# One more group of tokens by Strassen's products in a fused sliding attention and ReLU-squared kernel

## The chip, the cores and the metric

The kernel runs on one core of a Trainium2 chip. The metric is device time in microseconds of one execution; lower is better. Three runs of the kernel before gave 291.15, 291.99 and 292.82 us, a median of 291.99.

## The reference

Attention with a sliding window of 128 and a bias that falls off linearly with distance, over 8 batches, 8 heads, 576 positions and head size 64; then, on the 4608 tokens of 512 features that come out, a two-layer network with a squared ReLU between the layers.

```python
scores = scale * np.matmul(q, k.transpose(0, 1, 3, 2))
mask = (rel >= 0) & (rel < window)
scores = np.where(mask, scores + bias[None], -1000000000.0)
attn = np.exp(scores)
attn = attn / (np.sum(attn, axis=-1, keepdims=True) + 1e-09)
x = np.matmul(attn, v)
h = x @ w_in
r = np.maximum(h, 0.0)
g = r * r
return (g @ w_out).astype(np.float32)
```

## The kernel before

**Tiling.** The sequence of a batch is cut into 5 blocks of 128 positions (the last has 64), 40 blocks in all, numbered b0 to b39. A block's keys and queries are loaded as `kq`, turned by TensorE (`tp`, L483) or by a DMA into `kqT`, multiplied into scores (`ps_s`, L533 and L552), put through the exponential by ScalarE (`E`, L598), masked by VectorE (`P`, L609), multiplied with the values (`pv`, L639), normalised by VectorE (`rec`, `x`), and turned again (`xp`, L698) into `xT`, features by tokens. The 4608 tokens are also cut into 9 groups of 512. Group g can be worked on when its tokens stand in `xT`: group 1, tokens 512 to 1023, needs blocks b4 to b8.

**The network, direct form.** Up: `fc_step` (L745) multiplies slices of `w_in_sb` with the group's tokens into a bank `h`; ScalarE makes the ReLU `rt`, then VectorE or ScalarE the square `g`. Group 0 does so in slices of 128 tokens, group 1 in slices of 256 (`SPLIT`). Down: `plain` (L1054), for group 0 alone, 64 matmuls of 512 columns over `w_out_sb`.

**The network by Strassen's algorithm** (in the form with 7 products and 15 sums). The groups in `FAST`, 2 to 8, do their up-projection in `fast_unit` (L820): four units, one for each quarter of `w_in`, each with 7 products of 4 matmuls of 256 columns into banks `f`. It needs sums of quarters of `w_in` (`weight_sums`, L392: `w_sum`, made once) and of the group's tokens (`token_sums`, L789: `T`, and one of them in place in `xT`). In a unit ScalarE copies product 1 out (`fs`), VectorE adds that to product 6 in its bank (L886), ScalarE copies the sum out (`fu`), and only then may product 7 write that bank; it is copied out as `fx`. VectorE adds `fx` or `fu` to banks to give three quarters of the result (L854). Groups 1 to 8 do their down-projection so as well, in `product` (L975), with sums of quarters of `w_out` (`w_mix`, L377) and of `g` (`S`, L934).

**The order of the work** is made by a planner before the program is built. Each piece of work has a cost, the work it depends on, the buffers it takes and frees, and a key; the planner takes, engine by engine, what can start first, and by the key where several can. `SPREAD` shifts the keys by random draws. The engines then run their instructions strictly in that order. The keys of the first two groups count up from 0; of the loads, the order is written out in `FIRST` (b a block, i a quarter of `w_in`, o a quarter of `w_out`) and moved a little by draws with a negative share. POOL issues all loads (L429 blocks, L360 `w_in`, L367 `w_out`), SP all stores (L1043, L1021) and the transposes by DMA.

**The end.** For the last group the third result bank is two banks, one for each half of the rows, so that the last product (number 7, `halves`) can run one half after the other; each half has its addition (L1015) and its store of 128 x 256 (L1021).

## Time and profile before

| | us |
|---|---|
| median of three runs | 291.99 |
| the profiled execution | 291.18 |
| its span, first instruction to last | 289.2 |
| TensorE busy in the span | 281.6 |
| VectorE busy | 256.1 |
| ScalarE busy | 229.1 |
| POOL busy | 107.6 |

The page is one execution. Engines are PE (TensorE), PEld (its weight loads), DVE (VectorE), ACT (ScalarE), POOL and SP. A group of instructions has its line in the kernel, what it writes and reads, how many there are, their busy time, the mean duration of one in ns, and the idle time of the engine just before them with what ended it. Durations of neighbours on an engine can overlap by some tens of ns. The chain that ended last is followed back from the last instruction, at each step to what released it or to the instruction ahead of it on its engine.

### The profile page before, as it was taken

The page shows a single profiled execution, that of the slowest core. Times are in us where ns is not written, and L with a number is a line of the kernel's source. Part 1 is how long each engine was busy: PE and PEld are TensorE (multiplying, and loading weights), DVE is VectorE, ACT ScalarE, POOL GpSimd, SP SyncE. Part 2 cuts the span into 40 slices and gives each one's busy share as a digit, 9 for nine tenths or more (in the row PEclk, how much of TensorE's full clock was granted, in tenths as well). Part 3 has the DMA queues.
Part 4 walks back from the last instruction along what each step waited for, and adds up shares of the span by engine and source line. Part 5 has one row for each costly group of instructions (what it writes and reads, how often), then busy time and mean ns, then how long its engine had stood idle before and what let it go on. Part 6 is the DMA issues. An engine that isn't in the chain of part 4 may idle for free.

```text
span 289.2 us, 9480 instructions
## 1 busy us (share of the span) xinstructions
PE 281.6 (97%) x3869; PEld 239.2 (83%) x3869; DVE 256.1 (89%) x625; ACT 229.1 (79%) x470; POOL 107.6 (37%) x134
## 2 busy tenths in 40 slices
PE   8899999999999999999999999999999999999995
PEld 6788878865788888888988888888888888888884
DVE  6876879999798999998999999989999988998823
ACT  6659888995489985999899989898879888588420
POOL 8958676944672516332634245332000000000000
PEclk9999999999999999999999999999999999999999
DMA  9999999999999999999999999999234101201223
GB/s 135 160 179 174 172 180 186 155 126 208 191 191 141 150 126 192 161 161 110 226 158 126 127 197 157 164 177 158 37 101 70 47 20 61 86 0 39 74 75 109
DMA packets 165867, 38.36 MB, mean 133 GB/s; under 512 B 153024, under 2 KB 165312, under 8 KB 165824
## 3 DMA queue, kind: packets, MB, share of 16 engines
q0 software_dynamic: 114704, 18.10, 92.3%
q1 hardware_dynamic: 50064, 19.41, 35.8%
q8 instruction: 30, 0.49, 0.7%
q10 hardware_dynamic: 1056, 0.26, 0.4%
q14 instruction: 13, 0.11, 0.1%
HBM read 36.70 MB, written 9.44 MB: 160 GB/s over the span
## 4 chain that ended last, share of the span: by engine, by line
PE 88%; POOL 4%; DMA 3%; DVE 2%; ACT 1%; issue 0%; DVEq 0%
PE o L975 33%; PE f L820 30%; PE h L745 8%; PE pv L639 6%; PE o L1054 5%; DMA w_in_sb<-in_moe_w_in_dram 3%; PE ps_s L533 3%; POOL kq L429 2%; PE ps_s L552 2%; POOL vt L429 1%; PE tp L483 1%; POOL w_in_sb L360 1%; PE xp L698 1%; DVE rt L854 1%; DVE g L869 0%
## 5 line engine op out<-in xcount | busy, mean ns | idle before, releaser
L429 POOL DMA_DIRECT2D vt<-in_v_dram x40 | 34.1, 854 | 66.5 <-PE pv L639 58.1
L598 ACT ACTIVATE E<-ps_s 128x384 bf16<-128x384 f32 (+2 forms) x114 | 50.5, 508 | 8.6 <-PE ps_s L533 8.6
L975 PEld LDWEIGHTS <-g 128*128 128x128 bf16 x512 | 49.1, 98 | 6.0
L820 PEld LDWEIGHTS <-w_sum 128*128 128x128 bf16 x448 | 43.1, 97 | 6.3 <-issue 0.5
L609 DVE TENSOR_TENSOR P<-E,masks 128x1024 bf16<-128x1024 bf16 (+1 forms) x67 | 43.5, 656 | 2.5 <-ACT E L598 1.6
L429 POOL DMA_DIRECT2D kq<-in_k_dram x39 | 33.2, 851 | 24.9 <-DMA kqT<-kq 17.5
L975 PEld LDWEIGHTS <-S 128*128 128x128 bf16 x384 | 36.6, 98 | 4.5 <-issue 0.4
L848 ACT ACTIVATE rt<-f 128x512 bf16<-128x512 f32 x56 | 33.2, 600 | 6.8 <-PE f L820 6.6
L975 PE MATMUL o<-w_out_sb,g 128*128 128x256 bf16 x256 | 38.3, 273 | 0.0
L975 PE MATMUL o<-w_mix,g 128*128 128x256 bf16 x256 | 37.2, 273 | 0.0
L745 PE MATMUL h<-xT,w_in_sb 128*128 128x128 bf16 (+1 forms) x384 | 35.3, 237 | 1.2 <-issue 0.6
L975 PE MATMUL o<-w_mix,S 128*128 128x256 bf16 x256 | 36.1, 273 | 0.2 <-ACT E L598 0.2
L820 PEld LDWEIGHTS <-w_in_sb 128*128 128x128 bf16 x336 | 31.8, 97 | 4.4
L820 PE MATMUL f<-xT,w_in_sb 128*128 128x256 bf16 x224 | 34.6, 273 | 0.0
L429 POOL DMA_DIRECT2D kq<-in_q_dram x39 | 33.4, 857 | 2.6 <-PE h L745 1.3
L871 ACT ACTIVATE g<-rt 128x512 bf16<-128x512 bf16 x52 | 32.6, 634 | 1.7 <-DVE rt L859 0.9
L820 PE MATMUL f<-xT,w_sum 128*128 128x256 bf16 x224 | 33.5, 272 | 0.2 <-DVE rt L854 0.2
L672 DVE TENSOR_TENSOR x<-pv,rec 128x256 bf16<-128x256 f32 (+1 forms) x80 | 33.0, 415 | 0.4
L820 PE MATMUL f<-T,w_sum 128*128 128x256 bf16 x224 | 32.1, 273 | 0.0
L639 PE MATMUL pv<-vt,P 128*128 128x65 bf16 x576 | 30.8, 193 | 0.9 <-DVE P L609 0.9
L639 PEld LDWEIGHTS <-P 128*128 128x128 bf16 x576 | 25.7, 97 | 6.1 <-DVE P L609 2.0
L745 PEld LDWEIGHTS <-w_in_sb 128*128 128x128 bf16 x384 | 26.7, 98 | 3.7 <-issue 1.0
(78 smaller groups left out, 504.1 us busy)
## 6 DMA issues: line engine op xcount, KB each, us to landing
out_dram<-osb SPq DMA_DIRECT2D x35, 256.0 KB, 3.7
vt<-in_v_dram POOLq DMA_DIRECT2D x32, 128.0 KB, 5.5
kq<-in_k_dram POOLq DMA_DIRECT2D x31, 128.0 KB, 6.0
kq<-in_q_dram POOLq DMA_DIRECT2D x31, 128.0 KB, 6.3
w_out_sb<-in_moe_w_out_dram POOLq DMA_DIRECT2D x4, 512.0 KB, 9.6
w_in_sb<-in_moe_w_in_dram POOLq DMA_DIRECT2D x6, 256.0 KB, 7.9
kq<-in_k_dram POOLq DMA_DIRECT2D x8, 64.0 KB, 5.7
kq<-in_q_dram POOLq DMA_DIRECT2D x8, 64.0 KB, 6.2
```

Of the source, the lines that this page charges most:

```text
L429: nc.gpsimd.dma_start(o, src[b, :, kb * 128:kb * 128 + n, :].rearrange("h s d -> s h d"))
L533: nc.tensor.matmul(sl.tile[lo:lo + 64, at:at + w], k[rows, c, unit:unit + 64], own[rows, C + c, q0:q0 + w], start=True, stop=True)
L598: nc.scalar.activation(o, src, AF.Exp, bias=0.0, scale=scale)
L609: nc.vector.tensor_tensor(Pt[sP.idx][:, hs, p0:2, 0:n], e, masks[:, hs, p0:2, 0:n], op=ALU.mult)
L639: nc.tensor.matmul(slot_v.tile[:, hi * (D + 1):(hi + 1) * (D + 1)], Pt[sP.idx][:, place(h), part, :], vt[s_in[mk, "v"].idx][:, h, :], star ...
L672: nc.vector.tensor_tensor(xt[sx.idx][0:n, hf * 256:(hf + 1) * 256].rearrange("p (h e) -> p h e", h=4), pv[0:n, :, 0:D], srec.tile[0:n, :]. ...
L745: nc.tensor.matmul(slot.tile[:, f * w:(f + 1) * w], w_in_sb[:, cc, (fc + f) * 128:(fc + f + 1) * 128], xT[:, cc, g * 512 % RING + lo:g * 5 ...
L820: nc.tensor.matmul(bank[name].tile[:, jj * 256:jj * 256 + 256], w, m, start=opens and jj == 0 and k == 0, stop=k == 1, skip_group_check=True)
L848: nc.scalar.activation(srt.tile, bank[name].tile, AF.Relu, bias=0.0, scale=1.0)
L871: nc.scalar.activation(o, i, AF.Square)
L975: nc.tensor.matmul(bank[t].tile[:, t * 256:(t + 1) * 256], left(g, what, j)[:, t * 128:(t + 1) * 128], right(by, j), start=opens and j == ...
L1054: nc.tensor.matmul(bank.tile, g_slots[g].tile[:, fc, t * 128:(t + 1) * 128], w_out_sb[:, fc], start=fc == 0, stop=fc == FCB - 1)
```

## The change

Group 1 joins `FAST`: its up-projection takes the seven products too, 112 matmuls of 256 columns for 128 of 256. Its token sums and units stand at the keys where its `fc_step` calls stood, and the weight sums ahead of them, where before they stood behind group 0. A weight sum is one instruction of 512 columns; it was two of 256. For the last group the third result bank is three banks (of the planner's class `z` the third): rows 0 to 127 with 256 columns, rows 128 to 255 with two times 128 columns. Products 5 and 7, which write them, have 24 matmuls each for 16, product 7 piece after piece, and each piece has its addition and store. `SPREAD` has other draws, 14 for 11, so that work of all groups is ordered anew.

```diff
--- before.py
+++ after.py
@@ -227,7 +227,7 @@
     EARLY = 0.92
     WIDE = NKB
     SQUARES = 352.0
-    FAST = range(NG - 7, NG)
+    FAST = range(NG - 8, NG)
     RING = 4 * 512
     HALVED = (0, 1, 2)
 
@@ -265,7 +265,7 @@
 
     plan = Plan({"rec": 4, "rt": 3, "g": 2, "S": 2, "S2": 1, "osb": 4,
                  "s1": 1, "u2": 1, "x1": 1, "fs": 1, "fu": 2, "fx": 1, **size},
-                {"h": 3, "o": 3, "a": 4, "f": 5, "t": 3})
+                {"h": 3, "o": 3, "a": 4, "f": 5, "t": 3, "z": 1})
 
     def bank_tile(sl, name, dtype=FP32):
         return psum.tile([128, 512 if dtype == FP32 else 1024], dtype, tag=f"bank{sl.idx}", bufs=1, name=name)
@@ -388,9 +388,8 @@
         for o, a, b, op in ((s1, a21, a22, ALU.add), (s2, s1, a11, ALU.subtract),
                             (s3, a11, a21, ALU.subtract), (s4, a12, s2, ALU.subtract)):
             def emit(o=o, a=a, b=b, op=op):
-                for k in range(2):
-                    nc.vector.tensor_tensor(o[:, k], a[:, k], b[:, k], op=op)
-            last = plan.add({"DVE": 2 * dve(256, 2)}, key, emit, [t_win[n][-1], last, t_read[1][0]])
+                nc.vector.tensor_tensor(o, a, b, op=op)
+            last = plan.add({"DVE": dve(512, 2)}, key, emit, [t_win[n][-1], last, t_read[0 if 1 in FAST else 1][0]])
         t_wsum[n] = last
 
     s_in, t_in = {}, {}
@@ -958,7 +957,7 @@
     def product(g, i, key):
         what, by, where = PRODUCTS[i]
         if i == 0:
-            KEEP[g] = {"bank": [[Slot("o")] * 2, [Slot("o")] * 2, [Slot("o"), Slot("o")] if g == NG - 1 else [Slot("o")] * 2],
+            KEEP[g] = {"bank": [[Slot("o")] * 2, [Slot("o")] * 2, [Slot("o"), Slot("o"), Slot("z")] if g == NG - 1 else [Slot("o")] * 2],
                        "last": None, "t": [None] * 3,
                        "s1": Slot("s1"), "u2": Slot("u2"), "x1": Slot("x1")}
         kp = KEEP[g]
@@ -967,27 +966,32 @@
         apart = bank[0] is not bank[1]
         last = kp["last"]
         halves = i == 6 and g == NG - 1
-        for j, t in ([(j, t) for t in range(2) for j in range(FCB // 2)] if halves
-                     else [(j, t) for j in range(FCB // 2) for t in range(2)]):
-                def emit(j=j, t=t):
-                    if opens and j == 0 and (t == 0 or apart):
-                        bank[t].tile = bank_tile(bank[t], "o")
-                    nc.tensor.matmul(bank[t].tile[:, t * 256:(t + 1) * 256],
-                                     left(g, what, j)[:, t * 128:(t + 1) * 128], right(by, j),
-                                     start=opens and j == 0 and (t == 0 or apart), stop=j == FCB // 2 - 1,
+        parts = [(0, 0, 256), (1, 0, 128), (1, 128, 256)] if apart else [(0, 0, 256), (1, 0, 256)]
+        done_at = []
+        for j, x in ([(j, x) for x in range(len(parts)) for j in range(FCB // 2)] if halves
+                     else [(j, x) for j in range(FCB // 2) for x in range(len(parts))]):
+                t, lo, hi = parts[x]
+
+                def emit(j=j, x=x, t=t, lo=lo, hi=hi):
+                    if opens and j == 0 and (x == 0 or apart):
+                        bank[x].tile = bank_tile(bank[x], "o")
+                    nc.tensor.matmul(bank[x].tile[:, t * 256 + lo:t * 256 + hi],
+                                     left(g, what, j)[:, t * 128:(t + 1) * 128], right(by, j)[:, lo:hi],
+                                     start=opens and j == 0 and (x == 0 or apart), stop=j == FCB // 2 - 1,
                                      skip_group_check=True)
+                t = x
                 new = j == 0 and t == 0
                 here = [bank[t]] if opens and j == 0 and (t == 0 or apart) else []
-                end = i == 6 and j == FCB // 2 - 1 and t == 1
-                if halves and j == 0 and t == 1:
-                    half_done = last
+                end = i == 6 and j == FCB // 2 - 1 and t == len(parts) - 1
                 if what[0] == "s":
                     needs = [t_sum[g, j // 4]]
                 else:
                     needs = [q for lo, hi, q in g_sq[g][2 * j + (what != "a11")]]
-                last = plan.add({"PE": mm(256)}, key(i * 16 + 2 * j + t), emit,
+                last = plan.add({"PE": mm(hi - lo)}, key(i * 16 + 2 * j + t), emit,
                                 [last, (t_wmix if by[0] == "t" else t_wout)[j // 2], kp["t"][where] if new else None] + needs,
                                 here, [g_slots[g], s_slots[g][0]] if end else [s_slots[g][1]] if i == 1 and j == FCB // 2 - 1 and t == 1 else [])
+                if j == FCB // 2 - 1:
+                    done_at.append(last)
         kp["last"] = last
         k = key(i * 16 + 15)
 
@@ -1008,17 +1012,17 @@
                 copy(te, f32(so.tag, so, plan.bufs[so.tag]), bank[0].tile)
             te = plan.add({"ACT": act(512), "DVE": dve(512)} if i in BOTH else {"ACT": act(512)}, k, keep, [done_], [so], free)
         elif halves:
-            for t, dep in ((0, half_done), (1, last)):
+            for x, (t, lo, hi) in enumerate(parts):
                 so = Slot("osb")
 
-                def plus(t=t, so=so):
-                    nc.vector.tensor_tensor(f32("osb", so, plan.bufs["osb"])[:, 0:256], bank[t].tile[:, t * 256:t * 256 + 256],
-                                            kp["u2"].tile[:, t * 256:t * 256 + 256], op=ALU.add)
-                te = plan.add({"DVE": dve(256)}, k, plus, [dep, kp["from", "u2"]], [so], [bank[t], kp["u2"]])
-
-                def store(t=t, so=so):
+                def plus(x=x, lo=t * 256 + lo, hi=t * 256 + hi, so=so):
+                    nc.vector.tensor_tensor(f32("osb", so, plan.bufs["osb"])[:, 0:hi - lo], bank[x].tile[:, lo:hi],
+                                            kp["u2"].tile[:, lo:hi], op=ALU.add)
+                te = plan.add({"DVE": dve(hi - lo)}, k, plus, [done_at[x], kp["from", "u2"]], [so], [bank[x], kp["u2"]])
+
+                def store(t=t, lo=lo, hi=hi, so=so):
                     r0 = g * 512 + t * 128
-                    nc.sync.dma_start(out[r0:r0 + 128, 256:512], so.tile[:, 0:256])
+                    nc.sync.dma_start(out[r0:r0 + 128, 256 + lo:256 + hi], so.tile[:, 0:hi - lo])
                 plan.add({"SP": 350.0}, k, store, [te], [], [so], dma=1040.0)
             return
         else:
@@ -1026,11 +1030,11 @@
             add = kp[{4: "x1", 6: "u2"}[i]]
 
             te = None
-            for lo, hi in ((0, 256), (256, 512)) if apart else ((0, 512),):
-                def plus(lo=lo, hi=hi):
+            for x, (lo, hi) in enumerate(((0, 256), (256, 384), (384, 512)) if apart else ((0, 512),)):
+                def plus(x=x, lo=lo, hi=hi):
                     if lo == 0:
                         f32(so.tag, so, plan.bufs[so.tag])
-                    nc.vector.tensor_tensor(so.tile[:, lo:hi], bank[lo // 256].tile[:, lo:hi], add.tile[:, lo:hi], op=ALU.add)
+                    nc.vector.tensor_tensor(so.tile[:, lo:hi], bank[x].tile[:, lo:hi], add.tile[:, lo:hi], op=ALU.add)
                 te = plan.add({"DVE": dve(hi - lo)}, k, plus, [te, last, kp["from", add.tag]], [so],
                               free + [add])
         kp["t"][where] = te
@@ -1068,13 +1072,20 @@
 
     key = 0
     for g in range(2):
-        for lo, hi in SPLIT[g]:
+        if g in FAST:
+            for n in range(4):
+                weight_sums(n, key + 14 * n - 12)
+            t_of = token_sums(g, key)
+            for n in range(4):
+                fast_unit(g, n, key + 16 * n, t_of)
+            key += 64
+        for lo, hi in SPLIT[g] if g not in FAST else []:
             for fc in range(0, FCB, 512 // (hi - lo)):
                 fc_step(g, fc, key, lo, hi)
                 key += 4
     for g in range(NG):
         base = key
-        if g == 1:
+        if g == 1 and 1 not in FAST:
             for n in range(4):
                 weight_sums(n, base + 64 * n)
         if g and g + 1 in FAST:
@@ -1096,8 +1107,9 @@
             if g * 512 < lo + blk[kb] and g * 512 + 512 > lo:
                 t.deps += t_read[g]
 
-    SPREAD = ((78, 3, 1), (425, 16, 0.01), (451, 8, 0.01), (463, 8, 0.03), (537, 3, 0.1), (602, 1.5, -0.15),
-              (705, 3, 0.03), (1454, 16, 0.03), (1463, 3, -0.15), (1578, 3, 0.03), (1611, 3, 0.01))
+    SPREAD = ((9504, 3, 1), (9631, 8, 0.01), (9673, 8, 0.1), (9696, 3, 0.03), (9736, 8, 0.1), (9741, 3, 0.03),
+              (9777, 3, 0.03), (9891, 3, -0.15), (9976, 8, 0.03), (10008, 3, 0.01), (10013, 16, 0.03),
+              (10071, 3, 0.01), (10091, 16, 0.01), (10181, 16, 0.01))
     work_of = sorted({t.group for t in plan.tasks if t.group[1] > -100000})
     load_of = sorted({t.group for t in plan.tasks if t.dma and -900000 < t.group[1] < -800000})
     shift = dict.fromkeys(work_of + load_of, 0.0)
```

**The order, POOL, the loads after block b3.** Names: `w_in_sb` 128x4x512 is a whole quarter of `w_in`, here the last; `kq_71`, `vt_79` with 64 rows are b4, `kq_72`, `vt_80` are b5, `kq_73` b6. Before:

```order
L360 DMA w_in_sb<-in_moe_w_in_dram 128x2x512 x2
L429 DMA kq_71<-in_k_dram 64x8x64
L429 DMA kq_71<-in_q_dram 64x8x64
L429 DMA vt_79<-in_v_dram 64x8x64
L429 DMA kq_72<-in_k_dram 128x8x64
L429 DMA kq_72<-in_q_dram 128x8x64
L429 DMA vt_80<-in_v_dram 128x8x64
L360 DMA w_in_sb<-in_moe_w_in_dram 128x4x512
L429 DMA kq_73<-in_k_dram 128x8x64
```

Now:

```order
L360 DMA w_in_sb<-in_moe_w_in_dram 128x2x512 x2
L360 DMA w_in_sb<-in_moe_w_in_dram 128x4x512
L428 DMA kq_71<-in_k_dram 64x8x64
L428 DMA kq_71<-in_q_dram 64x8x64
L428 DMA vt_79<-in_v_dram 64x8x64
L428 DMA kq_72<-in_k_dram 128x8x64
L428 DMA kq_72<-in_q_dram 128x8x64
L428 DMA vt_80<-in_v_dram 128x8x64
L428 DMA kq_73<-in_k_dram 128x8x64
```

The last quarter of `w_in` moved ahead of the six loads of b4 and b5.

**The order, PE, behind the last transpose of block b8's result** (`xp` from `x_2_89`), with which group 1's tokens are complete. Before, group 1's direct matmuls follow:

```order
L698 LDWEIGHTS x_2_89
L698 MATMUL xp_1303<-ident_64,x_2_89 128x128
L745 LDWEIGHTS w_in_sb_66
L745 MATMUL h_1274<-xT_69,w_in_sb_66 128x256
L745 LDWEIGHTS w_in_sb_66
L745 MATMUL h_1274<-xT_69,w_in_sb_66 128x256
```

Now, matmuls of group 0's down-projection follow (`g_480` is group 0's `g`):

```order
L697 LDWEIGHTS x_2_89
L697 MATMUL xp_1276<-ident_64,x_2_89 128x128
L1058 LDWEIGHTS g_480
L1058 MATMUL o_1075<-w_out_sb_67,g_480 128x512
L1058 LDWEIGHTS g_480
L1058 MATMUL o_1075<-w_out_sb_67,g_480 128x512
```

Of group 0's 64 matmuls of 512 columns 42 now stand ahead of group 1's first product, and the eleventh behind this place is the first to need the last quarter of `w_out`. Before, 7 of the 64 stood ahead of group 1's first direct matmul, and the other 57 behind 104 or more of its 128.

**The order, DVE, around the normalisation of block b3** (`x_89`). Now weight sums stand among it; before, the first stood behind the first `w_mix`:

```order
L671 TENSOR_TENSOR x_89<-pv,rec 128x256
L661 RECIPROCAL rec<-pv 128x4
L391 TENSOR_TENSOR w_sum<-w_in_sb 128x2x256
L671 TENSOR_TENSOR x_89<-pv,rec 128x256
L766 TENSOR_TENSOR g<-rt 128x4x128
L391 TENSOR_TENSOR w_sum<-w_sum,w_in_sb 128x2x256
L442 COPY xT<-xp 128x4x128
L391 TENSOR_TENSOR w_sum<-w_in_sb 128x2x256 x2
```

The sums of the first quarters moved from the middle of group 1's direct form to the time of b3's attention.

## The prediction

> **What bounds the kernel now.** I read the page first, busy time and the 40 slices, then the chain that ended last, then that chain in order of time.
>
> ```profile
> PE 281.6 (97%) x3869; PEld 239.2 (83%) x3869; DVE 256.1 (89%) x625; ACT 229.1 (79%) x470; POOL 107.6 (37%) x134
> PEclk9999999999999999999999999999999999999999
> PE 88%; POOL 4%; DMA 3%; DVE 2%; ACT 1%; issue 0%; DVEq 0%
> ```
>
> TensorE is busy for 97% of the span at full clock and is 88% of the chain. A busy PE can still be slowed by pauses between pipelined matmuls, so I look at the pace inside long runs of the chain in order of time (start, length, what, how many):
>
> ```profile
> 29.10 1.34 PE h L745 x24
> 33.17 0.47 PE ps_s L533 x32
> 55.85 0.45 PE tp L483 x8
> 74.15 1.51 PE o L1054 x7
> 80.15 0.48 PE pv L639 x16
> 249.83 2.18 PE f L820 x20
> 270.07 15.62 PE o L975 x143
> ```
>
> A matmul of 256 columns takes 2.18 / 20 = 0.109 us, one of 128 columns 1.34 / 24 = 0.056, one of 512 columns 1.51 / 7 = 0.216, a transpose 0.056, a pv 0.030, a block's scores 0.47. The last 143 matmuls run at 15.62 / 143 = 0.109 without a gap. So PE is bound by its own work almost everywhere, and a matmul saved is worth its full 0.109 us, if what feeds PE keeps up. The second engine by load is VectorE. The stretches tell where each has room (us, then busy time with counts of PE, PEld, DVE, ACT, POOL, clock, DMA share, GB/s):
>
> ```profile
> 10.00:20.00 10.00, 9.25 (x194) 8.36 (x188) 7.12 (x19) 6.91 (x14) 7.31 (x10) 1.00 1.53 171
> 20.00:30.00 10.00, 9.52 (x210) 8.50 (x208) 7.26 (x18) 8.64 (x19) 8.63 (x11) 1.00 1.90 175
> 30.00:40.00 10.00, 9.37 (x202) 7.95 (x199) 7.83 (x23) 8.57 (x17) 6.92 (x9) 1.00 1.93 176
> 40.00:50.00 10.00, 10.00 (x160) 8.72 (x152) 8.95 (x27) 8.64 (x18) 6.18 (x8) 1.00 1.66 187
> 50.00:60.00 10.00, 10.00 (x150) 7.70 (x148) 10.00 (x37) 9.75 (x21) 8.99 (x11) 1.00 2.37 148
> 60.00:80.00 20.00, 20.00 (x257) 13.13 (x255) 17.62 (x51) 12.80 (x30) 9.35 (x12) 1.00 1.92 180
> 150.00:200.00 50.00, 49.78 (x708) 42.87 (x706) 48.90 (x114) 45.82 (x98) 18.33 (x22) 1.00 1.58 160
> ```
>
> Before 40 us PE has small holes while loads arrive; from 40 us it has none. VectorE is 98% busy from 150 to 200 us and PE still loses only 0.22 us there.
>
> **The eighth up-projection: PE.** Group 1 leaves the direct form, 128 matmuls of 256 columns, and takes Strassen's, 7 products x 4 units x 4 = 112 matmuls of 256 columns. The 16 that go are worth 16 x 0.109 = **-1.74 us**, the only large gain in the change.
>
> **The same: VectorE and ScalarE.** The forms with their mean durations (line, engine, operation, count | busy us, mean ns | idle before):
>
> ```profile
> L886 DVE TENSOR_TENSOR f<-f,fs 128x512 f32<-128x512 f32 x28 | 19.2, 687 | 1.4 <-ACT fs L880 1.4
> L854 DVE TENSOR_TENSOR rt<-f,fx 128x512 bf16<-128x512 f32 x28 | 19.2, 685 | 4.4 <-ACT fx L901 4.0
> L859 DVE TENSOR_SCALAR rt<-rt 128x512 bf16<-128x512 bf16 x28 | 9.2, 330 | 0.6
> L789 DVE TENSOR_TENSOR T<-xT 128x512 bf16<-128x512 bf16 x7 | 2.9, 418 | 0.0
> L392 DVE TENSOR_TENSOR w_sum<-w_in_sb 128x256 bf16<-128x256 bf16 x16 | 3.7, 280 | 0.0
> L880 ACT ACTIVATE fs<-f 128x512 f32<-128x512 f32 x28 | 17.0, 606 | 2.4 <-PE f L820 2.1
> L890 ACT ACTIVATE fu<-f 128x512 f32<-128x512 f32 x28 | 16.8, 599 | 3.6 <-DVE f L886 3.5
> ```
>
> Four units add 4 additions into the bank (0.687), 8 additions that make rt (0.685), some 3 more ReLUs of rt (0.330), and 4 token sums (0.418): 2.7 + 5.5 + 1.0 + 1.7 = 10.9 us, and about two squares more, 0.8. That is 11.7 us of VectorE, all between about 40 and 80 us. What goes from there are the weight sums, 32 x 0.280 = 9.0 us, which stand between 47 and 72 us. Net +2.7 us. The idle time of VectorE in those 40 us is 40 - 8.95 - 10.00 - 17.62 = 3.4, so it ends at 98%, as it is from 150 to 200 us. ScalarE gets 12 copies of 0.60, 7.2 us, and has 40 - 8.64 - 9.75 - 12.80 = 8.8 idle; that is covered.
>
> The price of a full VectorE is paid where PE waits for the chain copy fs, addition, copy fu: 0.606 + 0.687 + 0.599 = 1.89 us, before the bank may take product 7. Beside it stand products 5 and 2 (8 x 0.109 = 0.87) and whatever attention lies between. The lower bound is the 0.22 us that the like stretch from 150 to 200 loses; the upper one is one whole chain, 1.9, since the four units share what is between them. I take **+0.7**, nearer to the low end, because that stretch runs the same chains at the same load.
>
> **The weight sums, wider and sooner.** They are 16 of 512 columns now. By the token sums' row of the same size (418 ns) that is 6.7 us, ahead of 40 us, where VectorE idles 2.88 + 2.74 + 2.17 = 7.8 us. They cost nothing as long as these holes cover them. If a mask or a normalisation comes late behind them, each costs PE up to its own 0.42; I leave it at 0, with up to 1 in the range.
>
> **The loads.** All go through POOL's one queue, in order.
>
> ```profile
> w_in_sb<-in_moe_w_in_dram POOLq DMA_DIRECT2D x1, 512.0 KB, 7.3
> L367 POOL DMA_DIRECT2D w_out_sb<-in_moe_w_out_dram x4: 772/780/792, 26.6 to 39.3; - x4
> DMA to landing us min/median/max: 8.5/9.6/10.3
> 40.59 0.39 PE L483 MATMUL tp<-ident,kq 128*128 128x128 bf16 x4
> ```
>
> The last quarter of w_in passes six loads of blocks 4 and 5. Half a megabyte at 175 GB/s is 3.0 us, so these blocks land up to 3 us later. PE's cover: ahead of block 4's transposes stand, by the order of both, 159 of group 0's h matmuls in place of 128, 31 x 0.056 = 1.7 us. What is missing, up to 1.3 us, is not lost for good, because PE now meets a later gate. Group 0's down-projection (64 matmuls of 512 columns) stands ahead of group 1's first matmul, 42 of the 64, and needs all of w_out. In both orders the second half of block 8's transposes is at the same place; in the trace it starts at 40.59 and leaves PE free at 40.81. From there to the first matmul that needs w_out's last quarter stand 28 of 512 columns, 32 pv, one block's scores (and 0.1 to drain them) and 12 transposes: 6.05 + 0.96 + 0.57 + 0.67 = 8.25 us, so PE arrives at 49.1. That quarter is issued at 39.3 and lands 8.5 to 10.3 us later, at 47.8 to 49.6. The wait is 0 to 0.5; I take **+0.5**, because that load is the last of a full queue. Before, direct h matmuls filled this time, and nothing waited.
>
> **The last product in three pieces.**
>
> ```profile
> L1033 DVE TENSOR_TENSOR osb<-o,u 128x512 f32<-128x512 f32 x7 | 4.7, 674 | 0.0
> L1015 DVE TENSOR_TENSOR osb<-o,u 128x256 f32<-128x256 f32 x2 | 0.8, 424 | 0.6 <-PE o L975 0.6
> out_dram<-osb SPq DMA_DIRECT2D x2, 128.0 KB, 1.8
> ```
>
> For the last group, products 5 and 7 (L975) trade 16 matmuls of 256 columns for 32 of 128: 32 x 0.056 - 16 x 0.109 = **+0.05**. After the last matmul stands an addition of 128 columns; halving 512 to 256 saves 0.25, so halving again saves half of that, **-0.13**. The store behind it is 64 KB: between nothing saved and half of 1.8, I take **-0.15**, since fixed parts of a transfer stay.
>
> The Trainium skill speaks against these pieces: TensorE: Matmul & The Clock Gate, Back-to-back issue gap, puts a stream of load and matmul pairs at about 81 ns for 128 columns, and 131 for 512. The trace disagrees twice, with 56 and 216. By that figure the pieces would cost 32 x 0.081 - 16 x 0.109 = +0.85, an estimate from that page, in place of +0.05.
>
> **Sum.** -1.74 + 0.7 + 0.5 + 0.05 - 0.13 - 0.15 = -0.77 us. The profiled execution took 291.18 (span 289.2 and 2.0 around it), so its like would take 290.4. The median of the three runs, 291.99, is 0.8 above that execution; from it the sum gives 291.2. I forecast the middle, **290.8**.
>
> **Rivals.**
>
> 1. **The covers hold everywhere: faster.** The waits of 0.5 and 0.7 come to nothing: -1.97, and the new draws, which reorder all groups, may take away some of the waits in the later part. In the middle of the two starting points that is 291.6 - 2.0 = 289.6. For it: every matmul saved lies on PE's chain, and PE loses almost nothing at 98% VectorE. Against it: the gate at 49 us did not exist before.
> 2. **VectorE becomes the bound: slower.** Over the whole run it gets 11.7 more and 9.0 - 6.7 = 2.3 less, 9.4 us, while PE gets shorter. It decides if from 40 us on the additions come more than about one chain (1.9 us) behind PE: then what does not fit into 3.4 us is carried into stretches that are already 98% busy, and PE waits at every unit. If half of the 9.4 shows, +4.7 - 2.0 = +2.7: 294.3. Against it: ScalarE can take squares and ReLUs.
> 3. **PE is bound by the queue of loads until 50 us, so the matmuls saved are not seen**, as blocks 4 to 6 and then w_out arrive when they arrive: the saving of 1.74 shrinks to the tail's 0.2: 291.4. For it: loads arrive one behind another there. Against it: group 1's up-projection, where the saving is, lies behind that gate.
> 4. The pace of 81 ns for 128 columns, by the page's rule: 291.6; the rows of 56 ns speak against it.
>
> **How the numbers follow.** Chances: forecast 0.37, rival 1 0.38, rival 2 0.14, rival 3 0.09, rival 4 0.02. What a measurement of this kernel tells from no change is about 0.5%, 1.46 us, so faster is below 290.5 and slower above 293.4. The forecast's own range is 289.9 to 291.9, by the bounds of its two waits and the two starting points, and counts as the same, near the edge. With rivals 3 and 4 the same has 0.48, faster 0.38, slower 0.14. The range that leaves out 2 in 10 goes from 289.2, rival 1 with some of the later waits gone, to 292.7, part of rival 2's way.
>
> **What would show it.** In the changed profile PE should have some 3869 matmuls (16 fewer for f and h, 16 more for o), VectorE's busy time some 9 us more, the weight sums before 35 us. A wait of PE for w_out near 49 us shows the gate; PE's f waiting for ACT fu between 50 and 75 us shows the chain; if both are missing and the time is under 290, rival 1 holds. Busy VectorE of 10 in every stretch from 40 to 100 us with PE under 9.9 shows rival 2. The forecast is wrong at its root if a run of 20 f matmuls no longer takes 2.18 us, or if PE from 40 to 270 us loses more than 2 us.

## The result, and the profile after

The changed kernel takes 296.25 us (median of four runs, 295.77 to 297.06) against 291.75 for the kernel before on the same chip: a ratio of 1.0155 with an interval of 1.0126 to 1.0184. It is slower by 4.5 us. The forecast was 290.8, no change, and the time lies above its range.

The page of the changed kernel: span, busy time, VectorE's 40 slices, and the chain that ended last by engine and by line.

```profile
span 295.3 us, 9476 instructions
PE 283.9 (96%) x3862; PEld 239.2 (81%) x3869; DVE 266.0 (90%) x632; ACT 231.8 (78%) x477; POOL 107.8 (37%) x134
...
DVE  6797989899999999999999899989999988989823
...
PE 54%; DVE 19%; ACT 11%; DMA 7%; POOL 5%; issue 2%; ACTq 0%
PE o L978 24%; PE f L819 20%; DMA w_out_sb<-in_moe_w_out_dram 4%; DMA w_in_sb<-in_moe_w_in_dram 3%; DVE rt L853 3%; DVE P L608 3%; PE pv L638 3%; POOL kq L428 3%; PE o L1058 3%; ACT g L870 2%; DVE S L933 2%; DVE x L671 2%; DVE f L885 2%; ACT E L597 2%; POOL vt L428 2%
```

TensorE's part of the chain fell from 88% to 54%, and VectorE, which had 2%, has 19%. TensorE's busy share hardly moved (97% to 96%), so the page says who has become critical but not where. The stretches say where. Columns as in the prediction: us, length, then busy time and count of PE, PEld, DVE, ACT, POOL, then clock, DMA share, GB/s. First the kernel before, in two stretches that it was not shown in above:

```profile
40.00:57.00 17.00, 17.00 (x251) 14.58 (x243) 15.95 (x52) 15.39 (x32) 12.55 (x16) 1.00 1.98 174
57.00:86.00 29.00, 29.00 (x387) 20.28 (x384) 26.45 (x77) 21.15 (x45) 16.37 (x21) 1.00 1.88 179
```

and the same stretches of the changed kernel:

```profile
40.00:57.00 17.00, 15.60 (x191) 9.65 (x194) 14.90 (x40) 6.74 (x14) 12.20 (x15) 1.00 1.82 182
57.00:86.00 29.00, 26.68 (x417) 20.24 (x419) 28.48 (x69) 26.72 (x59) 15.48 (x19) 1.00 2.06 152
```

From 40 to 57 us PE has lost 1.4 us of busy time, and ScalarE works less than half of what it did (6.74 for 15.39): it has nothing to do. From 57 to 86 us PE has lost 2.3, VectorE has 0.5 us left of 29 and ScalarE 2.3. So there are two places, a hungry one and a crowded one.

PE's busy time hides part of the loss, since a matmul that drains alone still counts as busy. So I also followed how far PE lags: the start of a matmul, less the work of all matmuls ahead of it at the paces of the prediction (0.109 us for 256 columns, 0.056 for 128, 0.216 for 512, 0.030 for a pv, 0.015 to 0.024 for a score; 0.083 for each of the 28 warm-up matmuls, which only shifts the points). Some records are missing from the traces, and not evenly. All 64 weight loads of group 0's down-projection (512 columns) are there in each, but behind them the kernel before has 64 matmuls, the changed one 57 and e1 to e14 56 to 58, and the gaps lie between 37 and 76 us. Each would add its 0.216 us to the lag, 1.3 to 1.7 us in all, to every kernel but the one before. So one matmul is put back behind each weight load that has none (in e7 two of its `h` as well). With them the changed kernel has the 3869 that the prediction named, and the stretches above have some 0.2 us more of PE in the first and 0.4 in the second. Lag in us, at that much work done; e1 is the changed kernel profiled again:

| work done, us | 10 | 30 | 45 | 60 | 70 | 100 | lag added 30 to 45 | 45 to 60 | 60 to 70 |
|---|---|---|---|---|---|---|---|---|---|
| before | 6.96 | 9.52 | 9.86 | 10.15 | 10.38 | 11.74 | 0.34 | 0.29 | 0.23 |
| changed | 7.98 | 10.35 | 12.65 | 14.11 | 17.61 | 18.44 | 2.30 | 1.46 | 3.50 |
| e1 | 8.57 | 12.51 | 13.80 | 15.22 | 18.79 | 19.61 | 1.29 | 1.42 | 3.57 |

In the changed kernel 30, 45, 60 and 70 us of work are reached at 40, 58, 74 and 88 us, so the first of the three differences is the hungry place and the other two are the crowded one. About 1 us of lag is there at the start. The hungry place adds 1 to 2 us more than before (0.9 of the 2.30 falls right at the point 30, and e1 has 1.29), the crowded place 4.4, and from there the changed kernel loses no more than the one before. At 100 us of work it is 6.7 us behind; PE's saving of 1.74 us stands against that, which leaves 5.0 beside the 4.5 measured.

What happens in the first place concerns group 1's matmuls. Here is the plain form of the kernel before, in a view by shape from 36 to 45 us, and the Strassen form of the changed one, the products on sums of tokens, in the view of the bank's tile from 40 to 60 us (count, duration ns min/median/max, first and last start, shape):

```profile
L745 PE MATMUL h<-xT,w_in_sb 128*128 128x256 bf16 x28 | 4.0, 273 | 0.0
```

```profile
L819 PE MATMUL f<-T,w_sum x14: 272/273/273, 54.0 to 59.6; 128*128 128x256 bf16 x14
```

By 45 us the kernel before has done 28 of group 1's matmuls, on the first 256 of its 512 tokens (`SPLIT`). A unit of Strassen's form waits for the sums of tokens, which mix both halves, so it needs all 512; the first product on such sums starts at 54.0. Until then PE takes group 0's down-projection, and ScalarE waits for work. In the second place the waits, from 60 to 90 us (who waited for whom: us in total, times, longest):

```profile
PEld L638 <- DVE x L671: 1.4, 2, 0.9
...
PE pv L638 <- DVE x L671: 1.0, 2, 0.6
...
PEld L697 <- DVE x L671: 0.9, 2, 0.4
...
PE f L819 <- DVE x L671: 0.6, 1, 0.6
```

PE waits for VectorE's attention rows, and the chain in order of time (start, length, what) shows why these are late:

```profile
80.10 0.69 DVE P L608
80.79 0.60 DVE S L933
81.39 0.33 DVE xT L442
81.73 0.60 DVE S L933
82.32 0.34 DVE T L788
82.66 0.60 DVE g L933
83.26 0.34 DVE T L788
83.60 0.60 DVE S L933
84.20 0.34 DVE xT L788
84.53 0.33 DVE x L671
...
85.29 0.58 DVE P L608
85.87 0.34 DVE x L671
86.21 0.05 issue
86.26 0.42 PE pv L638 x8
```

In this chain VectorE runs without a gap. Sums for the next products (S, g, T) stand between two masks P, and the pv that PE waits for comes 6 us after the first of them.

### The profile page after: what moved, and what is told of

Its sections match the earlier page's. It is cut to its first block, busy times and chain, and to the rows that moved or that the text cites. A ratio compares the mean times of both kernels' runs of the same rounds, so it can differ in the third digit from the quotient of the medians.

```text
span 295.3 us, 9476 instructions
## 1 busy us (share of the span) xinstructions
PE 283.9 (96%) x3862; PEld 239.2 (81%) x3869; DVE 266.0 (90%) x632; ACT 231.8 (78%) x477; POOL 107.8 (37%) x134
## 4 chain that ended last, share of the span: by engine, by line
PE 54%; DVE 19%; ACT 11%; DMA 7%; POOL 5%; issue 2%; ACTq 0%
PE o L978 24%; PE f L819 20%; DMA w_out_sb<-in_moe_w_out_dram 4%; DMA w_in_sb<-in_moe_w_in_dram 3%; DVE rt L853 3%; DVE P L608 3%; PE pv L638 3%; POOL kq L428 3%; PE o L1058 3%; ACT g L870 2%; DVE S L933 2%; DVE x L671 2%; DVE f L885 2%; ACT E L597 2%; POOL vt L428 2%
## 5 line engine op out<-in xcount | busy, mean ns | idle before, releaser
L819 PEld LDWEIGHTS <-w_sum 128*128 128x128 bf16 x512 | 49.0, 98 | 8.1 <-issue 0.9
L847 ACT ACTIVATE rt<-f 128x512 bf16<-128x512 f32 x64 | 38.0, 599 | 9.0 <-PE f L819 7.4
L819 PEld LDWEIGHTS <-w_in_sb 128*128 128x128 bf16 x384 | 36.6, 97 | 6.3 <-issue 1.4
L819 PE MATMUL f<-xT,w_in_sb 128*128 128x256 bf16 x256 | 40.7, 272 | 0.6 <-DVE x L671 0.6
L870 ACT ACTIVATE g<-rt 128x512 bf16<-128x512 bf16 x61 | 38.4, 636 | 2.4 <-DVE rt L858 1.5
L819 PE MATMUL f<-xT,w_sum 128*128 128x256 bf16 x256 | 39.6, 272 | 0.4 <-DVE rt L853 0.2
L819 PE MATMUL f<-T,w_sum 128*128 128x256 bf16 x256 | 39.2, 273 | 0.0
L978 PE MATMUL o<-w_mix,S 128*128 128x256 bf16 (+1 forms) x264 | 37.9, 269 | 0.0
L868 DVE TENSOR_TENSOR g<-rt 128x512 bf16<-128x512 bf16 x67 | 27.8, 420 | 3.5 <-ACT rt L847 1.4
L853 DVE TENSOR_TENSOR rt<-f,fx 128x512 bf16<-128x512 f32 x32 | 21.9, 684 | 4.0 <-ACT fx L900 3.7
```

The source lines that it names most:

```text
L819: nc.tensor.matmul(bank[name].tile[:, jj * 256:jj * 256 + 256], w, m, start=opens and jj == 0 and k == 0, stop=k == 1, skip_group_check=True)
L847: nc.scalar.activation(srt.tile, bank[name].tile, AF.Relu, bias=0.0, scale=1.0)
L853: nc.vector.tensor_tensor(srt.tile, bank[name].tile, add.tile, op=ALU.add)
L868: nc.vector.tensor_tensor(o, i, i, op=ALU.mult)
L870: nc.scalar.activation(o, i, AF.Square)
L978: nc.tensor.matmul(bank[x].tile[:, t * 256 + lo:t * 256 + hi], left(g, what, j)[:, t * 128:(t + 1) * 128], right(by, j)[:, lo:hi], start=o ...
```

## The experiments

The order of rows is made by the planner, and anything that changes its tasks also deals the draws anew. So some runs below keep the changed kernel's order and only make work smaller, and others drop the draws or replace them, and compare partners. e1 to e8 ran on one chip, e9 and e10 on a second and e11 to e14 on a third, where the kernel before took 291.1 to 291.3, 292.6 and 291.6 us. So between these three sets the ratios to the kernel before are compared, not the times.

**e1, the changed kernel again.**

> The changed kernel once more, beside its variants. All theories: 296 us, 4 to 5 above the kernel before. Its second profile tells whether two things in the first one are of the program or of that execution: the load of w_in's second half that landed 1.2 us later than before (15.9 for 14.8), and block b8's queries that took 1.9 us in the queue where a like load takes 0.9. If they are of the program, b8's queries land at 42 again; if of the execution, near 41.

296.55 us, ratio 1.0170 (1.0128 to 1.0213). It is the base of the next three.

**e2, the second group's additions on 64 columns.**

```diff
-                    nc.vector.tensor_tensor(srt.tile, bank[name].tile, add.tile, op=ALU.add)
+                    w = 64 if g == 1 else 512
+                    nc.vector.tensor_tensor(srt.tile[:, 0:w], bank[name].tile[:, 0:w], add.tile[:, 0:w], op=ALU.add)
+                    if g == 1:
+                        nc.vector.memset(srt.tile[:, w:512], 0.0)
...
-            nc.vector.tensor_tensor(bank["B"].tile, bank["B"].tile, fs.tile, op=ALU.add)
+            nc.vector.tensor_tensor(bank["B"].tile[:, 0:w], bank["B"].tile[:, 0:w], fs.tile[:, 0:w], op=ALU.add)
```

> The changed kernel, same order, but group 1's additions into the bank and its additions that make rt work on 64 of 512 columns (rt's rest is set to zero), so its numbers are wrong for that group. That takes 12 x 0.6 us from VectorE between 50 and 86 us and gives back about 12 x 0.15 + 8 x 0.15, some 4 us less. Theory VectorE (its queue is the chain from 57 to 86 us): 3 to 4 us faster than the changed kernel, 292 to 293. Rival loads (PE lost its time before 53 us to late loads, and would wait for VectorE less than 1 us): no more than 1 us faster, 295 or more. Rival order (the new draws put work badly in all groups): no more than 1 us.

294.72 us, ratio 1.0132 (1.0070 to 1.0194): 1.8 us less than e1, half of what the theory wanted, and with intervals that overlap. In the traces the lag added from 45 to 60 us of work falls from e1's 1.42 to 0.71, so a part of the loss is VectorE's additions.

**e3, no wait for w_out's later quarters**, and **e4, both**.

```diff
-        w = w_out_sb[:, 4 * n:4 * n + 4, :].rearrange("p (j u) (n f) -> p j u n f", u=2, n=2)
+        w = w_out_sb[:, 0:4, :].rearrange("p (j u) (n f) -> p j u n f", u=2, n=2)
...
-                nc.tensor.matmul(bank.tile, g_slots[g].tile[:, fc, t * 128:(t + 1) * 128], w_out_sb[:, fc],
+                nc.tensor.matmul(bank.tile, g_slots[g].tile[:, fc, t * 128:(t + 1) * 128], w_out_sb[:, fc % 4],
```

> The changed kernel, same order, but group 0's down-projection and the sums of w_out read the first quarter of w_out in place of the second to fourth, so nothing before 86 us waits for these three loads; the loads are still made. PE waited 0.56 + 0.21 + 0.22 us for them. Theory VectorE: gate and VectorE stand one behind the other on the chain, so at most these 1.0 us come back, 295.2 to 296. Rival loads: the later landings of w_out (45.5, 47.9, 51.8) hold up the sums on VectorE too, and 2 to 3 us come back, 293.5 to 294.3.

> Both of the last two edits. Theory VectorE with the gate in series: the sum of both, 4 to 5 us faster than the changed kernel, 291 to 292. Rival loads: like without the gate alone, 293.5. If the two cover each other, less than the larger of the two plus 0.5.

e3 took 295.42 us (1.0143, 1.0094 to 1.0192), as the theory of VectorE had it, and e4 295.29 (1.0129, 1.0088 to 1.0170), 3 us above what it had. Neither VectorE's load nor the gate, nor both, gives back more than 1.8 of the 5 us, and the intervals of e1 to e4 all overlap. These runs keep an order of rows that was made for the long chains; whether that is why, e14 tests. In e3 the lag still grows by 2.7 us from 30 to 60 us of work (e1: 2.7), so the gate is not what fills that stretch with lag.

**e5, everything but the eighth group.** The changed kernel with the old draws and

```diff
-    FAST = range(NG - 8, NG)
+    FAST = range(NG - 7, NG)
```

(and one key of the last product kept below the next whole number, so that the old draws fall on the same work).

> The change without its first part: seven groups by Strassen, the second group's up-projection plain on halves of its tokens as before, the old draws; the wide sums and the last product in three pieces stay. Eighth-group theory (the Strassen form of the second group costs the time: TensorE loses the half-token products that it had from 41 us on, and the vector and scalar engines get the chains): 290 to 292, within 0.5% of before. Rival, the order theory (any re-dealt order of rows costs some us, or the pieces and the wide sums do): 293 or more.

291.82 us, ratio 1.0025 (0.9997 to 1.0053). The wide sums, where the old order has them, and the three pieces cost at most 0.5%, and bring nothing that can be seen. The loss came with the eighth group or with the draws.

**e6 to e8, without draws.** `SPREAD = ()` in the kernel before (e6) and in the changed one (e8); e7 is e6 with the second group in one piece:

```diff
-    SPLIT = ([(0, 128), (128, 256), (256, 384), (384, 512)], [(0, 256), (256, 512)])
+    SPLIT = ([(0, 128), (128, 256), (256, 384), (384, 512)], [(0, 512)])
```

> The kernel before with an empty list of draws, so that the planner's own keys alone set the order. It is the base for the next two. Eighth-group theory: draws are worth 1 to 2 us, so 292 to 294. Order theory: the draws are worth as much as the loss, 295 or more.

> As e6, and the second group's plain up-projection waits for all of its 512 tokens (one piece in the place of two of 256): no chain is added to any engine, only the early half is gone. Eighth-group theory with the early half as a part of it: 1.5 to 3 us over e6, and TensorE idle or behind by 53 us. Theory of the full vector engine alone: within 0.7 us of e6. Order theory: nothing can be said of it but that it moves.

> The changed kernel with an empty list of draws: with e6 the pair of eight against seven groups in the planner's own order. Eighth-group theory: 4 to 7 us over e6. Order theory (the new draws are what is bad): within 1 us of e6, and below the changed kernel's 296.3.

| run | us | ratio to before | lag added 30 to 45 | 45 to 60 | 60 to 70 |
|---|---|---|---|---|---|
| e6, seven groups, halves | 293.61 | 1.0087 (1.0059 to 1.0115) | 0.41 | 0.30 | 0.26 |
| e7, seven groups, whole | 294.79 | 1.0119 (1.0096 to 1.0142) | 1.48 | 0.22 | 0.23 |
| e8, eight groups | 297.38 | 1.0218 (1.0196 to 1.0239) | 1.07 | 1.74 | 3.73 |

In the planner's own order the eighth group, with the wide sums and the pieces that e5 prices, costs 297.38 - 293.61 = 3.8 us (4 to 7 were expected), so it is not the new draws. Asking all 512 tokens of a plain group 1 adds lag in the first place only (1.48 for 0.41), with no chain added to any engine; in run time that is 1.2 us, with intervals that overlap, and less than the 1.5 to 3 that were expected. The second place appears with the Strassen form alone: 5.47 us of lag from 45 to 70 us of work in e8, 0.56 in e6 and 0.45 in e7. From 60 to 90 us PE's weight loads wait in e8 for VectorE's masks P (2.8 us) and rows x (1.3), in e6 for P alone (1.1). The stretches 40 to 60 and 60 to 90 us show it in e6, e7 and e8, in that order:

```profile
40.00:60.00 20.00, 19.79 (x278) 16.27 (x274) 19.38 (x65) 19.46 (x40) 14.47 (x18) 1.00 2.02 173
60.00:90.00 30.00, 29.74 (x424) 21.56 (x426) 26.81 (x71) 22.00 (x47) 14.68 (x18) 1.00 1.87 166
```

```profile
40.00:60.00 20.00, 18.98 (x251) 10.58 (x254) 18.54 (x58) 13.08 (x28) 14.58 (x18) 1.00 1.96 171
60.00:90.00 30.00, 29.68 (x391) 20.30 (x388) 28.49 (x80) 25.00 (x54) 15.89 (x19) 1.00 1.85 166
```

```profile
40.00:60.00 20.00, 19.27 (x253) 12.98 (x248) 17.27 (x47) 11.16 (x26) 14.20 (x17) 1.00 1.94 184
60.00:90.00 30.00, 26.59 (x401) 20.38 (x399) 29.08 (x70) 26.85 (x59) 14.81 (x19) 1.00 1.96 153
```

ScalarE tells the first place best: 19.46 us of 20 with halves, 13.08 whole, 11.16 by Strassen. That work moves into the second stretch (22.00, 25.00, 26.85), and PE falls there from 29.7 to 26.6, but in e8 alone. (With the missing records PE has 30.0 in e6 and e7, and 26.6 in e8.)

**e9, all chains of the second group short, order kept.** As e2, and the three copies as well:

```diff
-            nc.scalar.activation(f32(fs), bank["A"].tile, AF.Copy)
+            nc.scalar.activation(f32(fs)[:, 0:w1], bank["A"].tile[:, 0:w1], AF.Copy)
```

(`fu` and `fx` likewise; w1 is 64 in the second group.)

> The changed kernel, order of rows untouched, with the second group's Strassen chains made short on both engines: the copies fs, fu, fx on ScalarE and the additions into and plus on VectorE work on 64 of 512 columns (the rest of rt is set to zero), so the second group's output is wrong in value. It takes off ScalarE 12 times some 0.35 us and off VectorE some 3.5 us between 53 and 90 us. Chain theory (the added work on the two engines together sets 60 to 86 us): 2.6 to 3.5 us back, 293.0 to 294.0, and TensorE's idle time between 75 and 88 us mostly gone. VectorE-alone theory: no more than e2 gave, 294.7. Half-token theory alone (all is lost by 53 us): 296.

294.96 us, ratio 1.0106 (1.0051 to 1.0160). The expectation of 293 to 294 was missed; by the ratio e9 would take 294.2 on e2's chip, and its interval overlaps that of e2, so that shorter copies help beyond e2 is not shown. One reason why not more comes back stands in its chain in order of time and in its waits from 60 to 90 us:

```profile
72.28 0.52 PE ps_s L532 x32
72.81 7.84 DMA kqT<-kq
80.65 0.05 issue
80.69 0.40 PE ps_s L551 x8
```

```profile
PE ps_s L551 <- DMA kqT<-kq: 1.7, 1, 1.7
```

With less work on VectorE, PE waits 1.7 us for a block's keys and queries, which a DMA turns from 72.81 to 80.65 (e2 has the same wait, 1.6 us). As I read it, that is the order's doing: loads and transposes start when buffers come free, and in this order they come free late. In the changed kernel, whose order this is, POOL's loads of values wait so from 60 to 90 us (us in total, times, longest):

```profile
POOL vt L428 <- PE pv L638: 10.9, 3, 7.2
```

Shorter chains do not bring the pv forward that stands behind other rows. But in the kernel before the same loads wait 5.3 us for pv and 3.9 for f in this stretch, so the wait alone does not show it. e14 tests it.

**e10, half of the second group plain, no draws.** Hidden blocks 0 to 7 of group 1 plain on halves of its tokens, blocks 8 to 15 by Strassen:

```diff
+            for lo, hi in SPLIT[g] if g == 1 else []:
+                for fc in range(0, 8, 2):
+                    fc_step(g, fc, key, lo, hi)
+                    key += 4
             t_of = token_sums(g, key)
-            for n in range(4):
-                fast_unit(g, n, key + 16 * n, t_of)
-            key += 64
+            for n in range(2 if g == 1 else 0, 4):
+                fast_unit(g, n, key + 16 * (n - (2 if g == 1 else 0)), t_of)
+            key += 32 if g == 1 else 64
```

> No draws, as e6 and e8; the second group's first 8 hidden blocks are plain on halves of its tokens (64 matmuls that can start on 256 tokens), and only the last 8 by Strassen. Two-part theory (the early half that is lost, some 1.2 us, and the chains, some 2.6): the early work is there again for half as long and half of the chains are gone, so 294.0 to 295.5, between e6 (293.6) and e8 (297.4). Theory that what costs is the whole group's sums of tokens and the Strassen form as such: 296.5 or more.

294.19 us, ratio 1.0069 (1.0047 to 1.0091), within the two-part theory's times: no slower than e6 (1.0087, intervals overlap) and 1.5% under e8 (1.0218). The lag it adds is 1.15, 0.64 and 0.23 us, so the crowded place is gone and a part of the hungry one stays. e10 leaves out the wait that keeps plain products from reading tokens after one of the token sums has been put in their place; e13 has it.

**e11 to e13, other draws**, found by trying lists against the planner's own order: 25 for eight groups (e11), 21 for seven with the wide sums and the pieces (e12), 18 for the half (e13, whose sums of tokens also wait for the plain products: `+ t_read.get(g, [])` among what `token_sums` depends on). **e14** is e9 without draws and with the short times told to the planner, so that the order is made for them.

> The changed kernel with another list of draws, 25 of them, found by trying lists against the planner's own order. Eighth-group theory: the draws move some of it, but the loss belongs to the group: 294.0 to 296.0, still slower than before by 1% or more. Order theory (the change was made with a poor list of draws): 292 or less.

> Seven groups by Strassen with the wide sums and the last product in three pieces, as e5, with a list of 21 draws found in the same way and the same time as e11's. It is the partner of e11. Eighth-group theory: 290.5 to 292.5 and 2.5 to 4 us under e11. Order theory: within 1 us of e11.

> The second group's first 8 hidden blocks plain on halves of its tokens, the last 8 by Strassen (as e10, but the sums of tokens, which are partly made in place, wait for the plain products, so all values are right), with 18 draws found in the same way. Two-part theory: half of TensorE's early work is back and half of the chains are gone, so 290.0 to 292.5, level with e12 or under it by up to 0.9 us (8 matmuls fewer by half of the 1.74). Theory that any Strassen form in this group costs 3 us: 293.5 or more.

> No draws; as e8, with the second group's copies fs, fu, fx and additions into and plus on 64 of 512 columns (the rest of rt set to zero, so the second group's output is wrong in value), and the planner told of their short times, so that the order of rows is made for them. Two-part theory: most of the 2.6 us that lie between e7 and e8 come back and the lost half stays, 294.0 to 295.5. Theory that the chains' work is not what costs: 296.5 or more.

| run | us | ratio to before | lag added 30 to 45 | 45 to 60 | 60 to 70 |
|---|---|---|---|---|---|
| e11, eight | 295.26 | 1.0105 (1.0074 to 1.0137) | 0.46 | 1.64 | 1.87 |
| e12, seven | 290.28 | 0.9956 (0.9929 to 0.9983) | 0.23 | 0.37 | 0.23 |
| e13, half | 290.13 | 0.9941 (0.9918 to 0.9964) | 0.34 | 0.35 | 0.23 |
| e14, short chains | 295.04 | 1.0110 (1.0076 to 1.0143) | 1.96 | 1.37 | 0.46 |

e11 - e12 = 5.0 us, for 2.5 to 4 expected: with draws found in one way the gap between eight and seven groups stays. (The profiled execution of e11 is its slowest, 297.23 us. By 30 us of work it lags 2.9 us more than e12's, which was not followed up; the two places add 3.7 us more than e12's, 0.5 of it from 70 to 80 us of work.) e14 is 1.1% under e8, some 3 us, and its lag is smaller in the second place alone: 0.46 for 3.73 from 60 to 70 us of work. The first is not smaller, 1.96 for 1.07. Its stretch, and those of e13:

```profile
40.00:60.00 20.00, 18.53 (x224) 12.50 (x226) 17.01 (x49) 10.02 (x24) 13.92 (x17) 1.00 1.94 180
60.00:90.00 30.00, 29.25 (x435) 22.95 (x435) 28.09 (x82) 26.31 (x62) 15.90 (x19) 1.00 1.77 155
```

```profile
40.00:60.00 20.00, 19.84 (x313) 14.75 (x314) 18.20 (x50) 15.58 (x33) 15.30 (x19) 1.00 2.03 171
60.00:90.00 30.00, 29.74 (x407) 23.27 (x407) 29.14 (x74) 24.32 (x52) 12.59 (x15) 1.00 1.89 154
```

With chains shortened and the order made for it, PE is back at 29.25 of 30 and still hungry from 40 to 60. With half of the early work kept (e13), both stretches are full, 19.84 and 29.74 (20.0 and 30.0 with the missing records), though VectorE has only 0.9 us idle in the second. e8 had as much, 0.9, and PE lost 3.4 us there. So it is not VectorE's busy time as such that costs. e12 and e13 take 0.4% and 0.6% less than the kernel before. Which of the two is better the runs do not tell, and the gain of either may be its draws alone.

## Why the prediction was wrong, step by step

- **"The 16 that go are worth 16 x 0.109 = -1.74 us"** fits the traces: from e6 to e8 the lag added between 30 and 70 us of work rises by (1.07 + 1.74 + 3.73) - (0.41 + 0.30 + 0.26) = 5.6 us, and 5.6 - 1.74 = 3.8 is what the run times show. The matmul itself was not priced wrongly.
- **"That is 11.7 us of VectorE, all between about 40 and 80 us ... Net +2.7 us. The idle time of VectorE in those 40 us is ... 3.4"** is the step that failed. The amount was right: VectorE's busy time rose by 266.0 - 256.1 = 9.9 us, for 9.4 in the prediction. The place was wrong. Nothing of it can start before the group's 512 tokens are there: the token sums (1.7 of the 11.7 us) run from 50.8 us, and all the rest falls behind 54 us, where the first copy starts (row below). What idles earlier, and what the weight sums free there, is no use to it. From 57 to 86 us VectorE had 29 - 26.45 = 2.6 us to give, and the weight sums left another 3.4 there, 6.0 for some 10.

```profile
L879 ACT ACTIVATE fs<-f x32: 588/599/652, 54.2 to 270.8; 128x512 f32<-128x512 f32 x32
L391 DVE TENSOR_TENSOR w_sum<-w_in_sb x8: 411/416/419, 16.9 to 30.1; 128x512 bf16<-128x512 bf16 x8
```

- **"The price of a full VectorE ... I take +0.7"** was 4.9: (1.74 + 3.73) - (0.30 + 0.26) from e6 to e8. Its upper bound, one chain of 1.9, counted what PE waits for within a unit. The waits are elsewhere: for P and x of the attention, which stand in VectorE's row behind sums. From 57 to 86 us the changed kernel gets through 10 of these x where the one before has 14. The engine serves two streams in a fixed order here, and the stream that was not changed pays. e14 gives most of this back when the chains are short and the order is made for them, e9 only a part of it in the old order.
- **"I take +0.5"** for the gate of w_out, and its upper bound of 0.5, stood in place of 0.7 (1.07 - 0.41) from e6 to e8, and of 1 to 2 us in the changed kernel. That 0.5 and 0.7 lie close is luck: the loss is not the gate's. The sentence behind it, "before, direct h matmuls filled this time, and nothing waited", named what had gone, but I priced only the one load that I saw next, and not that ScalarE and VectorE lose this work there and have it in the crowded place. From 40 to 60 us PE's wait for w_out is short (0.4 us, last row below), as are those for a block's queries (1.1 with the weight load), and e3 without the gate had the same lag. It is a lack of ready work, spread over many small waits (in e1 PE comes to the same transposes 1.3 us later and does not wait for the queries):

```profile
PEld L482 <- DMA kq<-in_q_dram: 1.1, 1, 1.1
...
PE tp L482 <- DMA kq<-in_q_dram: 0.7, 1, 0.7
...
PE o L1058 <- DMA w_out_sb<-in_moe_w_out_dram: 0.4, 1, 0.4
```

- **The weight sums** ran from 16.9 to about 30.5 us at 416 ns each, as said (418, and before 35 us). The three pieces did what was said, too: the addition behind the last matmul went from 424 to 291 ns (the row below), within 0.01 us of the -0.13, and the smaller store lands in 1.7 us for 1.8. e5 shows that neither can be seen in the time. The pace of rival 4 does not hold: the last 24 matmuls, 16 of them of 128 columns, take 1.93 us, which is 8 x 0.109 + 16 x 0.056 = 1.77 and 0.16 for the last to drain.

```profile
L1019 DVE TENSOR_TENSOR osb<-o,u x3: 291/292/425, 290.7 to 291.6; 128x128 f32<-128x128 f32 x2, 128x256 f32<-128x256 f32 x1
```

- **Rival 2**, VectorE becomes the bound, 294.3, had 0.14 and was right in kind. Its argument against, "ScalarE can take squares and ReLUs", failed because ScalarE fills as well, 26.72 of 29 us. The prediction's own test for it, VectorE at 10 in every stretch from 40 to 100 us and PE under 9.9, holds from 60 to 90 us, not before. The forecast's sign of being wrong at the root came too: from 40 to 270 us PE is idle for 4.4 us, for 0.4 in the kernel before.

```profile
60.00:90.00 30.00, 27.42 (x420) 21.21 (x422) 29.85 (x75) 27.09 (x59) 15.20 (x19) 1.00 2.08 148
```

  It lacked the hungry stretch, and its 294.3 was 2 us short. Rival 3, in which late loads only hide the saving, had the stretch but not the loss in it.
- **The new draws** are not the cause: as ratios to the kernel before, eight groups take 1.0218 with none, 1.0155 with these, 1.0105 with e11's; seven take 1.0087 (e6), 1.0025 (e5) and 0.9956 (e12). What they are worth, 1.1% or some 3 us between e8 and e11, is nearly as large as the effect that was asked about, and the prediction had it in rival 1 alone, as a gain.

What stays open: how the loss divides between the early half that went and the chains that came. e7 takes the early half alone and loses 1.1 us of lag and 1.2 us of run time; e14 has the chains short and 1.74 us less of matmuls, and lies where e7 does (1.0110 and 1.0119). But work that is not done in the hungry place is done in the crowded one, and no run has the chains with the early half kept whole.

## What to carry to other kernels

Before costing work against idle time, ask when its inputs are complete. An algorithm that mixes a whole tile gives up the start on half of it, and idle time ahead of that start is worth nothing, while the time behind it gets all of the added work. Where a planner deals an order anew, compare each variant with a partner whose order was made in the same way (none, or the same search), because the dealing alone moved these kernels by up to 3 us. Before comparing counts or lags of two traces, check that both have all records: here 6 to 8 missing matmuls looked like 1.3 to 1.7 us of lost time. And taking the change for half of the tile, so that the early half keeps the engines fed, avoided the loss here (e10, e13); whether it gains anything beyond its draws, no run shows.

## What the runs showed of the hardware

Two executions, e2's and e3's profiles, show TensorE's granted clock at half for 3.4 us, late in the crowded place. In e2 it is half from 82.0 to 85.4 us (the clock is the third number from the end; 0.65 is the mean of 1.4 us at half and 0.6 at full):

```profile
78.00:81.40 3.40, 1.44 (x31) 0.74 (x28) 3.31 (x9) 2.91 (x9) 0.59 (x1) 1.00 1.74 148
...
82.00:84.00 2.00, 2.00 (x12) 1.42 (x10) 2.00 (x7) 1.11 (x3) 2.00 (x3) 0.50 2.64 194
84.00:86.00 2.00, 2.00 (x33) 1.36 (x35) 1.64 (x5) 0.00 (x0) 1.93 (x3) 0.65 1.61 244
```

PE had been busy for 1.44 of 3.4 us, with no single wait over 1.8. In e3, where the clock falls at 81.6, it had been busy for more, 2.04 of 3.5; in e9 for 1.80, and there it kept its clock. First e3, then e9:

```profile
78.50:82.00 3.50, 2.04 (x41) 1.26 (x39) 3.49 (x11) 3.37 (x9) 0.66 (x2) 0.94 1.92 115
```

```profile
78.50:82.00 3.50, 1.80 (x41) 1.43 (x40) 3.50 (x8) 2.81 (x8) 0.48 (x1) 1.00 1.98 119
```

The Trainium skill (TensorE: Matmul & The Clock Gate, Part 1: The HAM clock gate) has the clock fall to half after an idle window of about 3.4 us; here it fell at the end of stretches of that length in which PE was busy for 42% and 58% of the time. How busy PE is in such a stretch does not decide it alone, since 51% in e9 did not bring it down; what else does, no run here tells. From 60 to 70 us of work e2 adds 4.74 us of lag and e4, with the clock at full, 3.09, so such a drop costs some 1.6 us here. The two executions are the slowest of their four: 297.64 us with 294.02 to 295.35 for the others in e2, 297.16 with 294.39 to 295.46 in e3.
